# Start of an attention-then-ReGLU kernel: the first k heads in fp32 from the sync engine, w_phi's second copy and batch 0's q by matmul, and a new written order

## The chip, the cores and the metric

The kernel runs on one core of a Trainium2 chip. The metric is device time in microseconds (us). The engines are TensorE (PE, with its weight loads shown as PEld), VectorE (DVE), ScalarE (ACT), GpSimd (POOL) and SyncE (SP). SP, ACT and POOL issue DMA transfers; POOL's can change the type on the way. "The clock" is TensorE's granted clock, 1.00 being full.

## The reference

```python
def phi(x):
    proj = np.einsum('bhsd,df->bhsf', x, w_phi)
    proj = proj - np.max(np.abs(proj), axis=-1, keepdims=True)
    return np.concatenate([np.exp(proj), np.exp(-proj)], axis=-1)
q_p, k_p = (phi(q), phi(k))
kv = np.einsum('bhsf,bhsd->bhfd', k_p, v)
z = np.sum(k_p, axis=2)
num = np.einsum('bhsf,bhfd->bhsd', q_p, kv)
den = np.einsum('bhsf,bhf->bhs', q_p, z)[..., None] + 1e-06
attn = num / den
# x = attn, heads side by side: 4608 tokens x 512
out = (np.maximum(x @ w_gate, 0.0) * (x @ w_val)) @ w_out
```

There are 8 batches, 8 heads, 576 tokens, head size 64 and 128 features in w_phi; the gate and value weights are 512 x 1536, w_out is 1536 x 512. All inputs and the output are fp32 in memory.

## The kernel before, in words

**Tiling.** The 576 tokens of a batch are 512 "full" tokens (four tiles of 128) and 64 "rest" tokens. Heads go in three groups j = 0, 1, 2 of 2, 3 and 3 heads. The rest tokens of k ride along with group 0; the rest tokens of q of two batches together form "mixed" tiles, which make up a ninth block of 512 tokens. Each of the nine blocks (g = 0 to 8) then goes through the FFN: 12 column blocks of value (fv) and gate (fg) with four matmuls of 512 columns each, the product (ga), and four output tiles (fo, three parts each).

**Attention of one batch.** k is turned so that the head size lies on partitions (kt on DVE; in batch 0 k0 on PE, a transpose by matmul, and k1 on DVE, which copies it out). It is projected by w_phi (kr, from the 32-row copy w32; in batch 0 k2, from the 64-row copy w64). From the projection in a bank ACT makes both exponentials (ke, two for each of four token tiles and each group: 24 a batch), DVE the largest absolute value (kx), ACT the factors from it (kk, kp), and POOL, in batch 0 also DVE, scales v by them (vs, vd; vr for the rest tokens, vo and vp for the column of ones). kv sums over tokens on PE (80 matmuls of 65 columns), kc or kd copies it out. q goes the same way (qt on DVE, qc or qs on PE with w32, qe on ACT, qx on DVE); qy, qz, qu and qw make a factor per token. nu is q's product with kv, and nt, nv, nr (DVE) and nx (POOL) scale and normalize it. x is turned by xp and xa in batch 0, by a DMA (xt) elsewhere. In block 0 the FFN's first eight column blocks go tile by tile (pv, pg, pa, pb: 16 matmuls of 128 columns), so that they can begin with the first tile.

**Order.** The order of all work is written out in the string ORDER, some 2,000 words such as `ke.0.1.2.0:2@kp0`: step ke with arguments (batch 0, group 1, tile 2, sign 0), in bank 2, in slot 0 of the buffers kp. Each word calls the function `do_<step>`, and an engine runs its own instructions in the order of the words. There are eight banks of 128 x 512 fp32. Nothing reorders at run time: an instruction that waits holds up what its engine has behind it, and a DMA that waits holds up its issuer.

**The start.** POOL loads k, q and batch 0's v (lk L417, lq L424, lm, lv), bf16 for k and q, then the FFN weights (wl L477: value and gate in thirds; wo L483). SP loads w_phi twice: wp (L373) as 32 rows of pairs for w32, wq (L379) as 64 rows for w64, each in fp32, which wc (L382) and wd (L385) cast on DVE. `zz` are matmuls of zeros (L408, 256 columns) with no use for the result; there are 62. `gt` is a tiny SP load that waits for k of batch 0's first heads. After gt, SP loads v of batch 1 (L459).

The first words of the order before:

```python
ms.0 ms.2 ms.3@vr0 lk.0.1 ms.6 wp wq ms.4@vr1 wd ms.5 lq.0.1 wc id if zz.37:0 k0.1:0 k1.1:0@kT0
zz.5:1 k2.1:0123 lk.0.2 ke.0.1.1.0:1@kp0 ke.0.1.2.0:2 ke.0.1.3.0:3 ke.0.1.0.0:0 qt.0.1@qT0
...
lm.1.0 lv.0.0 ke.0.0.3.1:3 ke.0.0.1.0:0 ke.0.2.0.0:4 lv.0.2 ke.0.0.0.1:2 kk.0.1.0 lm.1.1 wl.1.0
...
nx.0.0@xu0 ke.1.1.3.1:0@kp2 wl.1.1 ke.1.1.0.0:7 nu.0.1.0:2 nt.0.1.0:2@t2 nu.0.2.0:4 xp.0.0:1
```

Of the kernel before, what the change touches and what calls it, by code (L numbers as in the profile page):

```python
# [8 lines left out]
FP32 = mybir.dt.float32  # L9
BF16 = mybir.dt.bfloat16  # L10
AF = mybir.ActivationFunctionType
ALU = mybir.AluOpType
# [4 lines left out]
ms.0 ms.2 ms.3@vr0 lk.0.1 ms.6 wp wq ms.4@vr1 wd ms.5 lq.0.1 wc id if zz.37:0 k0.1:0 k1.1:0@kT0  # L17
zz.5:1 k2.1:0123 lk.0.2 ke.0.1.1.0:1@kp0 ke.0.1.2.0:2 ke.0.1.3.0:3 ke.0.1.0.0:0 qt.0.1@qT0
ke.0.1.3.1:3 kx.0.1.1:1@mk0 lk.0.0 kx.0.1.2:2 ke.0.1.2.1:2 ke.0.1.1.1:1 lm.0.1 zz.6:4 k0.2:4
k1.2:4@kT0 zz.7:5 k2.2:4567 ke.0.2.2.0:6@kp1 kx.0.1.3:3 ke.0.2.3.1:7 lm.0.0 lq.0.0 kx.0.1.0:0  # L20
kx.0.2.0:4@mk1 ke.0.1.0.1:0 lw.0.0 k0.0:2 k1.0:2@kT0 zz.7:1 k2.0:2013 kk.0.1.1@ek0 ke.0.2.1.1:5
qt.0.0@qT1 kx.0.2.3:7 ke.0.2.2.1:6 kx.0.2.2:6 kx.0.0.0:2@mk2 lv.0.1 ke.0.0.2.1:1@kp2 ke.0.2.1.0:5
lm.1.0 lv.0.0 ke.0.0.3.1:3 ke.0.0.1.0:0 ke.0.2.0.0:4 lv.0.2 ke.0.0.0.1:2 kk.0.1.0 lm.1.1 wl.1.0
kx.0.2.1:5 kp.0.2.1:7 ke.0.0.0.0:2 ke.0.2.0.1:4 lw.0.1 qs.0.1.0:6 kx.0.0.1:0 kx.0.0.3:3 qx.0.1.0:6
vs.0.1.1@vs0 kp.0.2.0:7 qs.0.0.1:5 qe.0.0.1.0:5@qp0 gt.0 lk.1.3 qs.0.0.2:2 lv.1.2 kx.0.0.2:1
ke.0.2.3.0:7 vp.2:7@vs1 kk.0.0.1@ek1 vs.0.1.0 ke.0.0.2.0:1 qs.0.0.0:4 wl.0.1 kk.0.0.0 ke.0.0.3.0:3
qx.0.0.0:4 qx.0.0.2:2 vo.0@vs2 vd.0.2.0:7 ke.0.0.1.1:0 qs.0.1.1:1 qe.0.0.1.1:5 qe.0.0.0.1:4@qp1
qx.0.1.1:1 qs.0.1.2:3 qe.0.1.2.0:3@qp2 qe.0.0.0.0:4 qs.0.0.3:0 qe.0.0.3.0:0@qp3 wl.0.0 qe.0.1.0.0:6
qs.0.1.3:4 qx.0.0.1:5 qe.0.0.3.1:0 vd.0.2.1:7 qe.0.1.0.1:6 qe.0.1.1.0:1 vr.0.0.0 vr.0.0.1 qy.0.0:5
qx.0.1.2:3 vr.0.1.0 qx.0.1.3:4 vr.0.1.1 kv.0.2:7 kc.0.2:7@kv0 vo.1 kv.0.1:6 qz.0.0:5@my0 qu.0.0@mz0  # L30
qw.0.0@cq0 qx.0.0.3:0 kt.1.1@kT0 nu.0.0.2:7 nt.0.0.2:7@t0 qe.0.1.3.1:4 qy.0.1:0 qz.0.1:0@my0
vs.0.0.1 kc.0.1:6 ku.1@kT1 vs.0.0.0 kv.0.0:5 qe.0.1.3.0:4 nu.0.0.1:6 nt.0.0.1:6@t1 kc.0.0:5
qe.0.0.2.0:2 qu.0.1@mz0 qw.0.1 qy.0.2:0 qe.0.1.1.1:1 nv.0.0.1:6@u0 qe.0.1.2.1:3 qy.0.3:4 nu.0.0.0:5
nt.0.0.0:5@t2 qe.0.0.2.1:2 nv.0.0.2:7 nv.0.0.0:5 nr.0.0@r0 nu.0.1.1:1 qz.0.2:0@my0 qu.0.2@mz0 lv.1.0
nt.0.1.1:1@t2 qz.0.3:4@my0 nu.0.1.2:5 qw.0.2 nv.0.1.1:1@u1 lq.1.2 nt.0.1.2:5@t0 kr.1.1:7630
nx.0.0@xu0 ke.1.1.3.1:0@kp2 wl.1.1 ke.1.1.0.0:7 nu.0.1.0:2 nt.0.1.0:2@t2 nu.0.2.0:4 xp.0.0:1
xa.0.0:1 nv.0.1.2:5 nv.0.1.0:2 wo.0 nu.0.2.1:5 nr.0.1@r0 nx.0.1@xu0 kx.1.1.3:0@mk2 wl.0.2 nu.0.2.2:2
lm.2.0 nt.0.2.1:5@t2 ke.1.1.3.0:0 nt.0.2.2:2@t0 nt.0.2.0:4@t1 ke.1.1.1.1:6 lm.2.1 qu.0.3@mz0
kx.1.1.2:3 pv.1.0:1 pa.1.0:1@val0 ke.1.1.1.0:6 nv.0.2.0:4@u1 nv.0.2.1:5 nv.0.2.2:2 nr.0.2@r0
pg.0.0:0 nx.0.2@xu1 kx.1.1.0:7 kx.1.1.1:6 qw.0.3 xp.0.1:1 nu.0.3.1:4 xa.0.1:1 ke.1.1.0.1:7  # L40
# [12 lines left out]
fv.0.10:0 va.0.10:0@val3 fv.0.11:2 lk.2.3 qe.1.0.0.1:5 va.0.11:2@val0 qx.1.0.1:3 kr.1.2:0476
kx.1.2.0:0@mk2 ke.1.2.3.0:6@kp1 pg.1.3:5 fg.0.11:2 kx.1.2.2:7 kx.1.2.3:6 qe.1.0.1.0:3 ke.1.2.1.1:4
kx.1.2.1:4 ke.1.2.2.0:7 qe.1.0.3.1:1 ku.2@kT1 ke.1.2.0.1:0 pb.1.3:5 kk.1.2.0@ek2 ke.1.2.2.1:7
fv.0.9:3 va.0.9:3@val1 fg.0.8:1 ke.1.2.1.0:4 wo.1 lv.2.3 ga.0.11:2 vr.1.0.0 qy.1.0:7 qz.1.0:7@my0
mt.0 fg.0.10:5 ga.0.8:1 kk.1.2.1 ke.1.2.0.0:0 vs.1.0.1 mc.0:4732 me.0.2.0:3 mx.0.3:2 me.0.0.0:4
qu.1.0@mz0 mx.0.2:3 me.0.0.1:4 vr.1.1.1 vo.1.0 kv.1.0:0 kc.1.0:0@kv1 ga.0.10:5 mx.0.0:4 qw.1.0@cq0
mx.0.1:7 vs.1.1.1 kv.1.1:1 me.0.2.1:3 kc.1.1:1 nu.1.1.0:0 nt.1.1.0:0@t2 fg.0.9:5 vo.1.2@vs1 lv.2.0
kt.2.1@kT0 vs.1.2.1 nu.1.0.0:1 me.0.3.1:2 ga.0.9:5 ke.1.2.3.1:6 nu.1.0.1:4 nu.1.1.1:3 nt.1.1.1:3@t0  # L60
nt.1.0.0:1@t1 vs.1.2.0 kv.1.2:6 nv.1.1.0:0@u0 nv.1.1.1:3 me.0.1.0:7 kt.2.0 lw.2.1 fo.0.1.0:5
kc.1.2:6 nu.1.0.2:6 nt.1.0.2:6@t0 nu.1.1.2:3 nt.1.0.1:4@t2 me.0.3.0:2 nu.1.2.0:2 nt.1.2.0:2@t3
nv.1.0.0:1@u1 me.0.1.1:7 lq.2.2 nv.1.0.2:6 nv.1.0.1:4 nr.1.0@r0 nv.1.2.0:2@u2 fo.0.1.1:5 fo.0.1.2:5
oc.0.1:5@ob0 nt.1.1.2:3@t2 nu.1.2.2:4 nt.1.2.2:4@t3 lw.2.0 nv.1.1.2:3 nr.1.1@r1 kr.2.0:2617
# [196 lines left out]
def kernel(  # L261
# [805 lines left out]
```

## Time and profile before

| | |
|---|---|
| three runs | 379.4, 379.1, 378.24 us; median 379.1 |
| the profiled execution: its time | 378.79 us |
| its span (first to last instruction) | 376.8 us |
| mean granted clock | 0.986 |
| busy: PE, DVE, ACT, POOL | 367.3, 296.3, 222.6, 161.4 us |
| DMA | 38.04 MB, mean 101 GB/s |
| FFN matmuls of 512 columns (L916, L977) | 1,220 recorded, 379 ns each from start to modelled end |
| ke (L563), 192 | 513 ns each |
| qe (L709), 128 | 632 ns each |

Matmuls are pipelined: a matmul of 512 columns is recorded with 379 ns, but the next one starts 216 ns later, so four of them take 0.86 us in the chain of waits. On ACT and DVE too, instructions in a row overlap a little; ten ke take 3.95 us together. The page's slices divide the span in 40 parts, each digit being the busy share in tenths. Windows give busy times of each engine in a stretch that one names. The chain of waits goes back from the last instruction, at each step to what released it. The time of an execution is a little more than its span; the 2.0 us around it are not part of the program's instructions.

### The profile page before, as it was taken

To read this page: it belongs to the slowest core of one execution; us is meant where nothing else is said; L and a number is where in the kernel's file an instruction comes from. 1 tells how busy PE (TensorE), PEld (TensorE's weight loads), DVE (VectorE), ACT (ScalarE), POOL (GpSimd) and SP (SyncE) were. 2 spreads that over 40 slices of the span, in tenths; PEclk is the share of its full clock that TensorE was granted. 3 is DMA by queue.
4 is the path that set the end of the run, shared out by engine and by line. 5 is a ranking of instruction groups with operands and counts; after the bars stand their busy time and mean duration, and the time that the engine had idled before them with its cause. 6 is when DMAs were issued, how large, how long until landed. Compare 5 with 4: busy or idle time off the path is not lost.

```text
span 376.8 us, 9181 instructions
## 1 busy us (share of the span) xinstructions
PE 367.3 (97%) x3591; PEld 197.2 (52%) x3591; DVE 296.3 (79%) x680; ACT 222.6 (59%) x539; POOL 161.4 (43%) x180
## 2 busy tenths in 40 slices
PE   8788999999999999999999999999999999999996
PEld 6457857546544645455435554464444644444443
DVE  3989999989996899989989898888876657642351
ACT  1988996998578544776586547755774400302111
POOL 7777595595477042581475233812341212200000
PEclk9859999999999999999999999999999999999999
DMA  9999999699954664289713944193400021301122
GB/s 126 235 200 220 148 176 152 112 129 143 122 118 58 147 72 113 57 138 91 103 64 37 189 120 99 35 155 92 86 28 3 2 70 57 91 22 29 28 57 111
DMA packets 90513, 38.04 MB, mean 101 GB/s; under 512 B 64230, under 2 KB 85734, under 8 KB 90470
## 3 DMA queue, kind: packets, MB, share of 16 engines
q0 software_dynamic: 33904, 15.23, 31.2%
q1 hardware_dynamic: 56422, 22.10, 27.7%
q8 instruction: 28, 0.46, 0.6%
q10 hardware_dynamic: 144, 0.13, 0.1%
q14 instruction: 15, 0.12, 0.1%
HBM read 37.95 MB, written 9.44 MB: 126 GB/s over the span
## 4 chain that ended last, share of the span: by engine, by line
PE 89%; DVE 5%; ACT 4%; DMA 2%; issue 0%; SPq 0%; DVEq 0%; ACTq 0%
PE bank L916 46%; PE bank L977 22%; PE bank L658 6%; PE bank L757 4%; PE bank L945 4%; PE bank L694 3%; ACT kp L563 2%; PE bank L511 2%; DMA w64f<-in_w_phi_dram 2%; DVE mk L571 1%; ACT qp L709 1%; PE bank L1006 1%; PE bank L898 1%; DVE u L788 1%; DVE maxq L717 1%; DVE t L778 1%
## 5 line engine op out<-in xcount | busy, mean ns | idle before, releaser
L563 ACT ACTIVATE kp<-bank 128x384 bf16<-128x384 f32 x192 | 83.2, 513 | 26.2 <-PE bank L511 15.0
L977 PE MATMUL bank<-wo,h 128*128 128x512 bf16 x420 | 98.3, 379 | 0.0
L937 DVE SCALAR_TENSOR_TENSOR h<-bank,val 128x512 bf16<-128x512 f32 x100 | 66.3, 681 | 29.8 <-PE bank L916 25.5
L916 PE MATMUL bank<-xTs,wg 128*128 128x512 bf16 x352 | 86.7, 379 | 0.0
L916 PE MATMUL bank<-xTs,wv 128*128 128x512 bf16 x352 | 86.2, 379 | 0.0
L800 POOL TENSOR_TENSOR xu<-u,r 128x512 bf16<-128x512 f32 x36 | 37.5, 1044 | 97.3 <-DVE r L796 92.4
L931 ACT CAST val<-bank 128x512 bf16<-128x512 f32 x70 | 41.6, 606 | 62.2 <-PE bank L916 50.8
L709 ACT ACTIVATE qp<-bank 128x512 bf16<-128x512 f32 x128 | 70.9, 632 | 10.1 <-DVE maxq L717 5.1
L618 POOL TENSOR_TENSOR vs<-vn,ek 128x780 bf16<-128x780 f32 (+3 forms) x40 | 53.0, 1338 | 37.8 <-ACT ek L580 35.1
L977 PEld LDWEIGHTS <-h 128*128 128x128 bf16 x420 | 39.1, 98 | 44.0 <-issue 0.9
L916 PEld LDWEIGHTS <-wv 128*128 128x128 bf16 x400 | 37.0, 98 | 43.2 <-issue 3.5
L916 PEld LDWEIGHTS <-wg 128*128 128x128 bf16 x400 | 37.4, 98 | 42.0 <-issue 1.8
L571 DVE TENSOR_REDUCE mk<-bank 128x3 f32<-128x384 f32 x96 | 49.0, 539 | 4.3 <-ACT kp L563 2.2
L717 DVE TRANSPOSE_TENSOR_REDUCE maxq<-bank 128x16 f32<-128x512 f32 x64 | 42.3, 692 | 3.5 <-PE bank L694 2.3
L986 ACT COPY ob<-bank 128x512 f32<-128x512 f32 x23 | 13.6, 593 | 37.5 <-PE bank L977 37.2
L788 DVE TENSOR_TENSOR u<-bank,t 128x195 f32<-128x195 f32 (+1 forms) x108 | 33.4, 330 | 1.9
L778 DVE TENSOR_TENSOR t<-bank,cq 128x195 f32<-128x195 f32 (+1 forms) x96 | 29.8, 327 | 5.0 <-PE bank L757 4.1
L757 PEld LDWEIGHTS <-qp 128*128 128x128 bf16 x512 | 24.1, 98 | 13.6 <-issue 2.0
L757 PE MATMUL bank<-kv,qp 128*128 128x65 bf16 x512 | 27.2, 194 | 1.2 <-ACT qp L709 0.8
L934 DVE CAST val<-bank 128x512 bf16<-128x512 f32 x30 | 20.2, 678 | 8.4 <-PE bank L916 8.3
L658 PEld LDWEIGHTS <-kp 128*128 128x128 bf16 x640 | 24.0, 101 | 3.7 <-DVE h L937 0.3
L658 PE MATMUL bank<-vs,kp 128*128 128x65 bf16 x512 | 24.2, 199 | 0.0
(88 smaller groups left out, 357.0 us busy)
## 6 DMA issues: line engine op xcount, KB each, us to landing
out_dram<-ob SPq DMA_DIRECT2D x31, 256.0 KB, 2.2
vn<-in_v_dram SPq DMA_DIRECT2D x24, 256.0 KB, 5.4
kn<-in_k_dram POOLq DMA_DIRECT2D x7, 512.0 KB, 6.4
qn<-in_q_dram POOLq DMA_DIRECT2D x7, 512.0 KB, 7.6
wg<-in_moe_w_gate_dram POOLq DMA_DIRECT2D x3, 512.0 KB, 8.5
wv<-in_moe_w_val_dram POOLq DMA_DIRECT2D x3, 512.0 KB, 10.0
wo<-in_moe_w_out_dram POOLq DMA_DIRECT2D x3, 512.0 KB, 8.7
out_dram<-ob SPq DMA_DIRECT2D x9, 128.0 KB, 2.4
```

Source lines behind the costliest of these rows:

```text
L563: nc.scalar.activation(kp_of(3 * b + j)[:, i, s].rearrange("p n f -> p (n f)"), bank[bk[0]][:, 0 : 3 * F], AF.Exp, scale=(1.0, -1.0)[s],)
L571: nc.vector.tensor_reduce(mk_of(3 * b + j)[:, :, i], bank[bk[0]][:, 0 : 3 * F].rearrange("p (n f) -> p n f", f=F), axis=AX.X, op=ALU.max, ...
L618: nc.gpsimd.tensor_tensor(vs_of(3 * b + j)[:, s, 0:n].rearrange("p n i e -> p (n i) e")[:, :, 0:e], src[:, lo:hi].rearrange("p h i e -> p ...
L658: nc.tensor.matmul(out_ps[:, h - lo, s, :], lhsT=lhsT, rhs=rhs, start=(at == 0), stop=(at == 2 * n * (C + 1) - 1),)
L709: nc.scalar.activation(qp_of(4 * b + i)[:, s, 4 * hq : 4 * hq + 4].rearrange("p h m -> p (h m)"), bank[bk[0]], AF.Exp, scale=(1.0, -1.0)[s],)
L717: nc.vector.tensor_reduce(maxq[:, :, i, 4 * hq : 4 * hq + 4].rearrange("p t h -> p h t"), bank[bk[0]].rearrange("p (h t u) -> p h t u", h= ...
L757: nc.tensor.matmul(bank[bk[0]][:, E * n : E * (n + 1)], lhsT=qp_of(4 * b + i)[:, s, h, :], rhs=kv_of(b)[:, h, s, :],)
L800: eng.tensor_tensor(xu_of(n).rearrange("p (h d) -> p h d", d=D), u_of(n)[:, :, 0:D], r_of(n).to_broadcast([P, H, D]), op=ALU.mult,)
L916: nc.tensor.matmul(bank[bk[0]], lhsT=w[:, dc, P * f : P * f + P], rhs=xT(g)[:, dc, :], start=(dc == 0), stop=(dc == NDC - 1),)
L931: nc.scalar.copy(val_of(NFC * g + f), bank[bk[0]])
L937: nc.vector.scalar_tensor_tensor(h2_of(g, f), bank[bk[0]], 0.0, val_of(NFC * g + f), op0=ALU.max, op1=ALU.mult)
L977: nc.tensor.matmul(bank[bk[0]], lhsT=h2_of(g, f)[:, P * t : P * t + P], rhs=wo_sb[:, f, :], start=(f == 0), stop=(f == NFC - 1),)
```

## The change

- **lf, cf, cg**: k of batch 0's heads 2 to 4 comes in fp32 by one SP DMA, the first on that queue, into the memory of the mixed block's x (not yet in use); DVE casts two heads to bf16 and ACT one. The POOL load lk.0.1 goes.
- **wr**: the 64-row copy of w_phi is loaded from ACT's queue and no longer from SP's.
- **sl, w1, wa**: the 32-row copy is no longer loaded. sl (DVE) writes a selection matrix from the identity; w1 (PE, two matmuls) picks the rows from w64 into a bank; ACT copies them to w32. This stands ahead of batch 1's first projection.
- **q0, q1, qb**: batch 0's q is turned by PE (8 transposes of 128 columns for four heads, copied out by DVE) and projected from w64 by one matmul of 512 columns per tile and half, where two matmuls with w32 did it. Its four token tiles now hold every fourth token, so the output rows of block 0 are written with a stride of four.
- **vq**: the scaling of v for the rest tokens, both signs in one POOL instruction (16 for 32).
- **zz**: 17, 3, 5 and 4 in place of 37, 5, 6, 7 and 7.
- **Order**: all words are in a new order, and some evictions change engine (va 69 for 70, vb 31 for 30, oc 26 for 23, oe 9 for 12, kc 17 for 19, kd 7 for 5). do_lu, do_qv, and do_wc's new form are defined and not called.

```diff
-    w32f = sb.tile([P, 2, F], FP32, name="w32f", tag="w32f")
+    sel = sb.tile([D, 2, P], BF16, name="sel", tag="sel")
...
-    def do_wp(bk):
-        nc.sync.dma_start(
-            out=w32f.rearrange("p a f -> p (a f)"),
-            in_=w_phi.rearrange("(r a) f -> r (a f)", a=2)[None].to_broadcast([4, R, 2 * F]),
-        )
+    def do_sl(bk):
+        nc.vector.tensor_copy(
+            sel.rearrange("d a (i r) -> d a i r", r=R),
+            ident[0:D, 0:D].rearrange("d (r a) -> d a r", a=2)[:, :, None, :].to_broadcast([D, 2, 4, R]),
+        )
+
+    def do_w1(bk):
+        for a in range(2):
+            nc.tensor.matmul(
+                bank[bk[0]][:, F * a : F * (a + 1)],
+                lhsT=sel[:, a, :],
+                rhs=w64[0:D, :],
+                start=(a == 0),
+                stop=(a == 1),
+            )
...
+    def do_wr(bk):
+        nc.scalar.dma_start(out=w64f, in_=w_phi[None].to_broadcast([2, D, F]))
...
+    def do_wa(bk):
+        nc.scalar.copy(w32.rearrange("p a f -> p (a f)"), bank[bk[0]][:, 0 : 2 * F])
...
+    def k_first():
+        flat = xT_mix.rearrange("p a b -> p (a b)").bitcast(FP32)[:, 0 : 3 * C * D]
+        return flat.rearrange("p (h x) -> p h x", h=3)
+
+    def do_lf(bk):
+        lo, hi = HEADS[1]
+        nc.sync.dma_start(
+            out=k_first().rearrange("p h (c d) -> p h c d", d=D),
+            in_=k[0, lo:hi, 0:SF, :].rearrange("h (p c) d -> p h c d", c=C),
+        )
+
+    def cast_first(copy, half):
+        lo, hi = ((0, 2), (2, 3))[half]
+        at = HEADS[1][0]
+        copy(
+            kn_of(0)[:, at + lo : at + hi].rearrange("p h c d -> p h (c d)"),
+            k_first()[:, lo:hi],
+        )
+
+    def do_cf(bk, half):
+        cast_first(nc.vector.tensor_copy, half)
+
+    def do_cg(bk, half):
+        cast_first(nc.scalar.copy, half)
...
+    def do_vq(bk, b, hh):
+        r = slice(SM * hh, SM * (hh + 1))
+        nc.gpsimd.tensor_tensor(
+            vr_of(b)[r, :, :, hh, :],
+            vm_of(b)[r][:, None, :, :].to_broadcast([SM, 2, 4, E]),
+            ek_of(3 * b)[r, :, 0, :][:, :, :, None].to_broadcast([SM, 2, 4, E]),
+            op=ALU.mult,
+        )
...
+    def do_q0(bk, hq):
+        pt = bank[bk[0]].bitcast(BF16)
+        for n in range(8):
+            h, cp = 4 * hq + n // 2, n % 2
+            nc.tensor.matmul(
+                pt[:, P * n : P * n + P],
+                lhsT=qn_of(0)[:, h, 2 * cp : 2 * cp + 2, :].rearrange("p c d -> p (c d)"),
+                rhs=ident,
+                is_transpose=True,
+            )
+
+    def do_q1(bk, hq):
+        nc.vector.tensor_copy(
+            qT_of(hq).rearrange("p h m a -> p (h m a)"), bank[bk[0]].bitcast(BF16)
+        )
...
+    def do_qb(bk, hq, i):
+        T = qT_of(hq).rearrange("p h m a -> p (h m a)").rearrange("p (h k m) -> p h k m", k=2, m=P)
+        r = slice(D * (i % 2), D * (i % 2 + 1))
+        nc.tensor.matmul(bank[bk[0]], lhsT=w64[r, :], rhs=T[r, :, i // 2, :], start=True, stop=True)
...
             dst = out[S * g + P * t : S * g + P * (t + 1), :]
+            if g == 0:
+                dst = out[0:SF, :].rearrange("(p c) n -> p c n", c=C)[:, t]
```

The start of the new order, up to the first gate matmuls (lines in between left out):

```python
ms.0 id if ms.3@vr0 lf ms.4@vr1 ms.5 wr ms.2 cf.0 wd sl cg.1 lk.0.2 zz.17:0 k0.1:0 k1.1:0@kT0 zz.3:1
k2.1:0123 ke.0.1.0.1:0@kp0 ke.0.1.3.1:3 ke.0.1.0.0:0 ms.6 k0.2:4 kx.0.1.1:1@mk0 k1.2:4@kT0
ke.0.1.2.1:2 kx.0.1.3:3 kx.0.1.0:0 lq.0.0 ke.0.1.1.0:1 lm.0.0 ke.0.1.3.0:3 zz.5:5 k2.2:4567
...
qe.0.0.1.0:6 qz.0.0:3@my0 qu.0.0@mz0 kv.0.2:7 kt.1.1@kT0 qy.0.3:6 kc.0.1:1@kv0 lq.1.2 vo.0 vs.0.0.0
qe.0.0.3.0:5@qp3 kv.0.0:2 qz.0.3:6@my0 qw.0.0@cq0 qu.0.3@mz0 nu.0.0.1:1 kc.0.2:7 nt.0.0.1:1@t0
kc.0.0:2 qy.0.1:3 qz.0.1:3@my0 qe.0.1.2.1:0 qu.0.1@mz1 qe.0.1.3.0:4 qe.0.1.2.0:0 nv.0.0.1:1@u0
wl.1.0 nu.0.0.2:7 nu.0.0.0:2 nt.0.0.0:2@t1 nu.0.1.1:6 qw.0.1 w1:3 wa:3 nt.0.0.2:7@t0 nv.0.0.0:2
...
qe.0.0.3.1:5 nu.0.1.2:0 nt.0.1.2:0@t2 nv.0.1.0:2@u1 qe.0.1.3.1:4 zz.4:7 kr.1.1:1375 nv.0.1.2:0
...
xp.0.1:1 qw.0.3 ke.1.1.2.0:7 qt.1.1@qT1 xa.0.1:1 lv.1.1 pv.0.0:0 lv.1.3 pa.1.0:4@val0 lm.1.0
kx.1.1.2:7 pv.0.1:1 ke.1.1.1.0:3 nx.0.2@xu0 pa.0.0:0@val1 pa.0.1:1@val2 kt.1.0@kT0 nu.0.3.1:4
nt.0.3.1:4@t0 ke.1.1.3.0:5 pg.0.1:2 pb.0.1:2 qc.1.1:1065 wl.0.2 ke.1.1.1.1:3 ke.1.1.2.1:7 ln.0.1
```

More of the change, by code (lines that the diff above doesn't have):

```diff
@@ L462, in do_lv, with do_lu @@
             )
+    def do_lu(bk, i):
+        lo, hi = HEADS[i]
+        nc.sync.dma_start(
+            out=v_flat()[:, lo:hi],
+            in_=v[0, lo:hi, 0:SF, :].rearrange("h (p c) d -> p h c d", c=C),
+        )
     def do_gt(bk, j):
```

472 lines of the change are left out of this document (231 added, 241 removed).

## The prediction

> **What bounds the kernel now.** I read the 40 slices of the page first, then the windows, then the chain of waits, then the timeline of the first 10 us.
>
> ```profile
> PE   8788999999999999999999999999999999999996
> ...
> PEclk9859999999999999999999999999999999999999
> DMA  9999999699954664289713944193400021301122
> ```
>
> One slice is 9.4 us. TensorE (PE) is full from the fifth slice on; before it PE is not full and its clock drops to half in the third. The windows put numbers on that:
>
> ```profile
> 29.90:89.10 59.20, 58.71 (x839) 38.52 (x841) 57.05 (x144) 52.97 (x132) 44.43 (x50) 1.00 1.02 149
> 89.10:373.65 284.55, 284.50 (x2516) 142.95 (x2514) 216.87 (x488) 149.10 (x355) 95.49 (x97) 1.00 0.46 81
> ```
>
> The columns are length, then busy time of PE, PE's loads, VectorE (DVE), ScalarE (ACT) and GpSimd (POOL), clock, DMA. From 29.90 (the first batch-1 projection, step kr.1.1) to 373.65 (the last matmul) PE is busy 343.21 of 343.75 us. DVE, 57.05 of 59.20, is the second limit up to 89.10. So the end is the moment when this run begins, plus 343.75, plus 3.15 (to the end of the span at 376.8). Only the 29.9 us ahead can shrink; the rest can only grow. The chain of waits says what orders the start:
>
> ```profile
> 1.56 6.35 DMA w64f<-in_w_phi_dram
> 9.72 3.95 ACT kp L563 x10
> 13.77 3.06 ACT kp L563 x8
> ```
>
> First w_phi's 64-row copy is awaited till 7.91; then the exponentials of k go back to back on ACT, which is full (10.00 of 10 us between 10 and 20) and 8.69 of the next 10. The first exponential, 9.72, is therefore the handle. What lies between 7.9 and it:
>
> ```profile
> 7.65 0.50 PE L533 MATMUL bank<-ident,kn 128*128 128x128 bf16 x6
> ...
> 7.94 0.23 DVE L385 CAST w<-w64f 128x128 bf16<-128x128 f32 x1 [4.60 <-DMA w64f<-in_w_phi_dram]
> ...
> 8.22 0.35 DVE L382 CAST w<-w32f 128x256 bf16<-128x256 f32 x1
> 8.49 0.21 DVE L391 CAST identf<-ident 128x128 f32<-128x128 bf16 x1
> 8.62 0.54 DVE L536 COPY kT<-bank 128x768 bf16<-128x768 bf16 x1
> ...
> 9.23 0.51 PE L554 MATMUL bank<-w,kT 64*128 64x128 bf16 x12 [0.53 <-DVE kT L536]
> ```
>
> The first k was there in time (its transposes at 7.65 show no DMA wait), but DVE stands at w64f and has three more steps (a memset and two casts) ahead of the copy of kT.
>
> **Start of k (lf, cf, cg, wr, sl).** Removed: the w32f DMA of 128 KB and the first k DMA on POOL, two steps of DVE (0.35, and identf's 0.21 moved into idle time). Added: lf, 3 heads x 512 x 64 x 4 B = 384 KB, first on SP (0.74). Its landing was never seen in this form. Lower end: output stores of 256 KB take 2.2 us to land, x1.5 = 3.3, so 4.0. Upper end: v by SP into xTs takes 7.6 us for 256 KB under full load, x1.5 = 11.4, so 12.1. Nearest row: the same 384 KB of k, by POOL, issued at 1.25, beside w_phi and q; the kn row gives 4.7 us as the shortest of four (the next, 7.0, would end at 8.25, after the transposes began), so 5.95. I take 5.0 for lf, landing at 5.8 (estimate): q's 512 KB no longer run beside it, but the k of heads 5 to 7 soon does. wr, 64 KB on the empty ACT queue, lands before that; d1's ACT store of 128 KB takes 1.7.
>
> The Trainium skill, "Trainium Kernel Development and Optimization", Key Constraints, holds that DMAs from SP, ACT and POOL run on the same 16 engines and that several issuers save issue time only. The DMA row above (nine tenths from the first slice) agrees; by it the landing would be POOL's 5.95 less half a microsecond of earlier issue, 5.4 (an estimate), and the sum below -1.8 instead of -1.4.
>
> Then cf.0 on DVE: 128 columns take 0.23 and 256 take 0.35, so 512 take 0.60: 6.4; cg.1 (256 columns, ACT's 0.37) lies beside it. wd and sl (0.23 and about 0.3) lie beside the six transposes. These take 0.50 and the projection 0.51 at full clock; at half clock I add 0.25 to each. Which clock? The next windows are 3.41 us each:
>
> ```profile
> 2.90:6.31 3.41, 3.41 (x18) 2.35 (x16) 0.43 (x1) 0.00 (x0) 3.33 (x8) 1.00 1.12 170
> ...
> 13.14:16.55 3.41, 1.59 (x20) 0.70 (x19) 3.41 (x8) 3.41 (x11) 1.53 (x2) 1.00 1.04 228
> 16.55:19.96 3.41, 2.97 (x9) 0.59 (x10) 3.10 (x7) 3.41 (x14) 3.37 (x5) 0.50 1.20 195
> ...
> 23.38:26.79 3.41, 3.41 (x65) 3.41 (x64) 3.05 (x6) 2.17 (x6) 2.92 (x4) 0.50 1.23 203
> ```
>
> The clock fell to 0.50 after a window busy for 1.59, stayed there through one of 2.97, and came back after a full one (3.41), at 26.79. The opening zero matmuls go from 37 to 17; 16 loads fall into the first of these windows, 0.21 us each, so 17 end at 1.06 + 3.6 = 4.7, and the PE idles for lf until 6.4. I expect half clock there. So: 6.4 + 0.75 + 0.54 (copy of kT) + 0.76 = 8.45 for the first exponential, 1.27 earlier (1.77 at full clock).
>
> **Batch 0 after that.** The number of exponentials is unchanged (24 of k, 16 of q), so ACT keeps the gain if it is fed. K of heads 5 to 7 was issued at 3.51 behind q; now it is POOL's first DMA, behind the identity. On DVE the two transposes of q (1.10 and 1.09) become two copies of 1024 columns (0.54 x 4/3 = 0.73 each): 0.7 saved. On PE 16 matmuls of 512 columns become 8 and 16 transposes of 128: 3.5 to 2.6 us at 0.216 and 0.056 each, which lies beside full ACT, worth 0; uncovered it would be 0.9. Of DVE's 0.7 I count 0.3, since DVE and ACT both were nearly full up to 28. Added at the edge of the full run: two matmuls of w1 (0.11), 4 zero matmuls (0.44), and wa on ACT (0.37); kr.1.1 waits for wa, and ACT's queue and the exponentials of batch 1 stand behind it. I count 0.2 of them. Sum at the start: -1.27 - 0.3 + 0.2 = -1.4 us.
>
> **Elsewhere, 0.** vq: 16 POOL products of twice the width for 32 of 0.62 us; the 128x520 product takes 1.06, so 17 for 19.6 us, on an engine that waits 92 us for DVE's r alone. Evictions change engine: DVE gets one val and two kv more, three ob and two others fewer, about -1.6 us; ACT gets about 1.5 more, which its 149 of 284 busy us hide; in the stretch to 89.10 they would show. Batch 0's output rows are strided by 4 but are still 2 KB each. No instruction is dropped by "no bank kept". From kr.1.1 on the steps are the same, apart from those named; their order is new throughout.
>
> **DMA and queues.** SP: lf, then gt.0 and vm and four loads of v behind it, as before. POOL issues the first gate weights (wl.1.0) only after the last product of v, about 23.9 (25.42 less 1.5), instead of at 12.41; with 8.5 us to landing that is 32.4. Their first user, pg.0.1, follows pv.1.0 (about 32.2 - 1.4 = 30.8) after some 3 us of PE work, 33.8. 1.4 us of cover; beyond that PE stands, in order, microsecond for microsecond.
>
> **Sum.** The profiled execution has a span of 376.8 and a time of 378.79 (2.0 around it); -1.4 gives 377.4. The median of the three runs, 379.1, lies 0.3 higher and gives 377.7. I say **377.5**. About 0.3% (1.14 us) is what a measurement can tell from no change.
>
> **Rivals.**
> - *k lands early*: lf at 4.0, by the store row. First exponential at 6.65, 3.1 earlier: 375.7. Against it: DMA is full from the first slice. Chance 0.10.
> - *Gain eaten on the way*: wl.1.0 lands like wv's 10.0 instead of 8.5, at 33.9, and DVE (96% busy up to 89) holds the new order up for the rest; or lf, sharing its engines with wr and the k of heads 5 to 7, lands at 7.0 and the first exponential stays at 9.7. About 378.9. For it: 1.4 us of cover is thin. 0.27.
> - *Half clock in the full run* (slower): the 80 matmuls of kv take 4.4 us at half clock (55 ns each, from the timeline), so they fill a whole counting window only if they begin less than 1.0 us ahead of its edge. In the trace they began at 23.3, 0.1 before one. If they miss it, and PE between is under the 2.97 that did not restore it, half clock lasts up to two windows of full work, 6.8 us, and costs half, 3.4: net +2.0, 381.1. It decides at a loss of over 2.5 us. 0.15. The Trainium skill, "TensorE: Matmul & The Clock Gate", Part 1, says that the window is 3.4 us and free-running, not tied to the kernel's start; the spacing of the windows above agrees, and the phase cannot be predicted.
> - *lf late*: as v into xTs; landing at 10, first exponential 12.65, 2.9 later: 382. Slower by 0.3% from a landing at 9.7. 0.08.
>
> **Chances.** Forecast 0.40, early 0.10, eaten 0.27, half clock 0.15, late 0.08. Faster 0.50, same 0.27, slower 0.23. The range leaves out half of the early case and most of the late one: 375.6 to 381.2; the forecast's own is 376.6 to 378.0.
>
> **What would show it.** lf's landing (DVE's wait ahead of cf) at 5.8; first exponential at 8.45; half clock from the start till after kv; PE full from about 30.5 with no wait for wg; PE busy over 99.5% from there to the end; the same 3.15 us of tail. It is wrong if PE has idle time over 1.5 us after 31, or if the first exponential is not ahead of 9.

## The result, and the profile after

The kernel after takes 381.7 us (median of 19 runs, 379.95 to 383.78), the kernel before 378.95 (19 runs beside them, 378.16 to 380.0): 1.0065 times as long, 95% interval 1.005 to 1.0081. It is slower by some 2.5 us, where 377.5 and faster was forecast. The profiled execution has a time of 381.75 and a span of 379.9 us. One execution of a run below (e1), at 423.8 us with a mean clock of 0.84, was slow throughout and is left out of its median.

The slices of the page of the kernel after, one 9.5 us:

```profile
PE   7598998969999999999999999999999999999996
...
PEclk9689999999999999999999999999999999999999
DMA  9999899690966946596075295014442002200132
```

The half clock has moved from the third slice to the second. But the seventh and ninth slices of PE, nines before, are 8 and 6. Windows from the first batch-1 projection (kr.1.1, now at 26.92) to the last matmul, cut at the same distance as before (columns as in the prediction's: length, busy PE, PE's loads, DVE, ACT, POOL, clock, DMA share and rate):

```profile
26.92:86.12 59.20, 52.90 (x777) 35.01 (x777) 51.99 (x131) 47.84 (x120) 32.91 (x38) 1.00 0.98 147
86.12:376.88 290.76, 290.22 (x2568) 145.85 (x2566) 220.98 (x496) 154.88 (x370) 104.04 (x96) 1.00 0.44 81
```

So the sum of the prediction can be filled in: 26.92 + 349.96 + 3.07 = 379.95, where it was 29.88 + 343.77 + 3.13. The start gained 2.96 us, the dense stretch (from the first batch-1 projection to the last matmul) lost 6.19, the tail is as it was. The gain at the start is that of one execution: in the traces of five runs below whose words are the same up to there (e2, e3, e5, e7, e10), this projection came at 27.11 to 28.02, and with the start of before (e4, e14) at 29.84, so the gain is 1.8 to 3.0 us. PE is busy 343.1 us in the dense stretch now and was 343.2 before; what was added is waiting, with 52.90 of 59.20 us busy in the first window. PE's four longest waits behind 28.5 us (total, times, longest):

```profile
PE bank L996 <- issue: 3.2, 1, 3.2
PE bank L1025 <- DVE t L858: 1.4, 1, 1.4
PE bank L558 <- DVE kT L547: 1.3, 1, 1.3
PE bank L996 <- ACT ob L1066: 0.5, 1, 0.5
```

Together they are 6.36 us, where the trace of before had one of 0.35 in this stretch. The names to the right of the arrow are only the last to be seen; behind each stands a DMA. The profile gives the times from the issue of these DMAs to their landing:

```profile
wg<-in_moe_w_gate_dram POOLq DMA_DIRECT2D x1, 512.0 KB, 11.2
km<-in_k_dram POOLq DMA_DIRECT2D x1, 32.0 KB, 6.3
kn<-in_k_dram POOLq DMA_DIRECT2D x1, 512.0 KB, 7.4
xTs<-xu SPq DMA_TRANSPOSE x1, 5.9
```

- **wg**, the first third of the gate weights, sent at 22.55, landed at 33.72; PE stood from 32.36 to 33.77.
- **km**, batch 2's key tails (lm.2.1 at 54.95, lm.2.0 at 57.46), landed at 63.75; the turn ku.2 began at 63.84, and PE stood from 62.95 to 64.21 for kr.2.0. Before, these two loads had gone out at 34.19 and 34.91, thirty us ahead of their use at 64.4.
- **xTs**, the last transposed tile of batch 1 (xt.1.3), sent at 73.04, landed at 78.89; PE stood from 75.77 to 78.98 for the first products of FFN group 1. Beside it **kn**, batch 3's keys, had gone out on POOL at 72.87. Before, the same transpose took 2.44 us (71.08 to 73.52), with the keys sent two us behind it.
- The fourth: a store of an output tile (od.0.2) behind two transposes on SP, sent 115.70, landed 119.50; ScalarE waited for its buffer and PE 0.48 us for ScalarE.

The chain of waits of the kernel after passes through three of them (start, length):

```profile
54.95 8.80 DMA km<-in_k_dram x2
...
64.21 0.57 PE bank L558 x24
...
77.51 1.47 issue
78.98 3.18 PE bank L996 x14
...
115.70 3.79 DMA out_dram<-ob
```

At 77.51 it says "issue", where the times above show the landing at 78.89 behind the wait.

The start, VectorE's and ScalarE's timeline of the kernel after:

```profile
4.06 0.66 DVE L451 CAST kn<-xTm 128x512 bf16<-128x512 f32 x1 [0.16 <-DMA xTm<-in_k_dram]
5.52 0.40 DVE L400 CAST w<-w64f 128x128 bf16<-128x128 f32 x1 [0.80 <-DMA w64f<-in_w_phi_dram]
...
5.97 0.53 DVE L583 COPY kT<-bank 128x768 bf16<-128x768 bf16 x1
```
```profile
7.05 3.17 ACT L610 ACTIVATE kp<-bank 128x384 bf16<-128x384 f32 x8 [2.58 <-PE bank L601]
```

The fp32 keys were there at 4.04, w_phi's copy was what DVE awaited, until 5.52, and the first exponential came at 7.05, 2.67 us ahead of before.

### The profile page after: what moved, and what is told of

It reads as the page before. It is cut to its first block, busy times and chain, and to the rows that moved or that the text cites. A ratio compares the mean times of both kernels' runs of the same rounds, so it can differ in the third digit from the quotient of the medians.

```text
span 379.9 us, 9112 instructions
## 1 busy us (share of the span) xinstructions
PE 362.8 (95%) x3568; PEld 193.6 (51%) x3568; DVE 295.9 (78%) x679; ACT 224.2 (59%) x543; POOL 157.7 (41%) x163
## 3 DMA queue, kind: packets, MB, share of 16 engines
HBM read 37.81 MB, written 9.44 MB: 124 GB/s over the span
## 4 chain that ended last, share of the span: by engine, by line
PE 82%; DMA 5%; DVE 5%; ACT 4%; POOL 2%; issue 2%; SPq 0%; POOLq 0%; DVEq 0%; ACTq 0%
PE bank L996 45%; PE bank L1057 19%; PE bank L714 5%; PE bank L837 3%; PE bank L1025 3%; ACT kp L610 3%; DMA km<-in_k_dram 2%; PE bank L558 2%; PE bank L774 2%; DMA qn<-in_q_dram 2%; DVE u L868 1%; DVE t L858 1%; DMA out_dram<-ob 1%; DVE mk L618 1%; DVE qT L765 1%
## 5 line engine op out<-in xcount | busy, mean ns | idle before, releaser
L1011 ACT CAST val<-bank 128x512 bf16<-128x512 f32 x69 | 40.6, 597 | 65.1 <-PE bank L996 46.1
L789 ACT ACTIVATE qp<-bank 128x512 bf16<-128x512 f32 x128 | 69.9, 626 | 11.8 <-PE bank L774 7.6
L1066 ACT COPY ob<-bank 128x512 f32<-128x512 f32 x26 | 15.3, 594 | 38.9 <-PE bank L1057 29.7
L1014 DVE CAST val<-bank 128x512 bf16<-128x512 f32 x31 | 21.2, 682 | 7.1 <-PE bank L996 6.0
## 6 DMA issues: line engine op xcount, KB each, us to landing
wg<-in_moe_w_gate_dram POOLq DMA_DIRECT2D x3, 512.0 KB, 11.2
```

The lines of the kernel that those rows point to most:

```text
L789: nc.scalar.activation(qp_of(4 * b + i)[:, s, 4 * hq : 4 * hq + 4].rearrange("p h m -> p (h m)"), bank[bk[0]], AF.Exp, scale=(1.0, -1.0)[s],)
L1011: nc.scalar.copy(val_of(NFC * g + f), bank[bk[0]])
```

## Experiments

All are timed against the kernel before, in the same job.

| run | what | median us | ratio to before, 95% |
|---|---|---|---|
| e1, e7 | after, km early | 381.7, 381.9 | 1.0067 (1.0051 to 1.0083), 1.0080 (1.0063 to 1.0097) |
| e5 | after, keys of batch 3 early | 378.70 | 0.9992 (0.998 to 1.0004) |
| e2 | after, both | 377.74 | 0.9960 (0.9948 to 0.9972) |
| e3 | e2, store early, gate product later | 377.54 | 0.9962 (0.9947 to 0.9977) |
| e4 | before, km late | 383.22 | 1.0120 (1.010 to 1.014) |
| e14 | before, keys beside the transpose | 379.53 | 1.0004 (0.9988 to 1.0021) |
| e10 | after, wait filled | 382.82 | 1.0094 (1.0075 to 1.0112) |
| e6 | e2, first keys by POOL | 378.67 | 0.9993 (0.9985 to 1.0002) |
| e12 | e6, table loaded early | 378.74 | 0.9981 (0.9968 to 0.9995) |
| e11 | before, w_phi early, fewer fillers | 378.59 | 0.9981 (0.997 to 0.9993) |
| e8, e9, e13 | new start, old dense order | 388.9, 382.4, 382.0 | 1.0263 (1.0241 to 1.0286), 1.0081 (1.0059 to 1.0103), 1.0069 (1.0041 to 1.0096) |

### The waits of the new order, undone one by one

e1 moves two words of the order, e2 a third as well, e3 a pair and one store besides:

```diff
 e1   ... wl.1.2 ku.1 ...
+lm.2.1 lm.2.0
 lk.2.3 ...                          (both taken from behind wo.2)
 e2   ... lq.2.2 ... ku.2
+lk.3.3
 lm.3.1 ...                          (taken from behind nx.1.3, xt.1.3)
 e3   ... xp.0.2:3
+pg.0.1:2 pb.0.1:2                   (taken from ahead of qc.1.1)
 ...
+od.0.2
 xt.2.3 ...                          (taken from behind xt.2.2)
```

> The kernel after, with one thing moved: the two loads of batch 2's key tails (km) go out on POOL ahead of the load of batch 2's keys at about 40 us, instead of at 54.95 and 57.46. Theory A (single late landings): in the kernel after, TensorE waited 1.26 us at 62.95 for the first scores of batch 2, because km landed at 63.75; that wait goes, the scores start near 63, and the last normalised tile of batch 1, which ScalarE and VectorE reach sooner too, shortens the next wait (3.21 us at 75.77) by one to two more. Median 379.4, between 378.6 and 380.5. Theory B (the engines behind TensorE are the bound from 64 to 77): the idle time only moves to 75.8, and the median stays at 381.3 to 381.9.

> As the run before, and the load of batch 3's keys (1 MB read, 512 KB written) moved on POOL from 72.87, where it ran beside the last transposed tile of batch 1 on the way to TensorE (issued 73.04, landed 78.89, 5.85 us where others took 2.4 to 4.4), to about 60.6, right behind the load of batch 2's queries. Theory A: that tile lands some 3 us after its issue, and the wait of 3.21 us at 75.77 goes whole: median 377.2, between 376.5 and 378.5. Theory B: the tile is late because its normalisation (POOL, 71.88) is late, and at most 1 us more than in the run before comes off: 379 or over.

> As the run before, with two more: the store of an output tile that stood on SP behind two transposes (issued 115.70, landed 119.50, TensorE waiting 0.48 us at 119.73) goes ahead of them at about 110; and the first gate product of the first FFN part (which waited 1.41 us at 32.36 for its weights, landed 33.72) goes on TensorE behind a query product and a transpose that have their inputs by then (0.57 + 0.22 us). Theory A: 0.48 and up to 0.8 come off: median 376.0, between 375.3 and 377.5, faster than the kernel before. Theory B: no more than 0.3 comes off.

e1 gained nothing, as theory B had it. e2 gave 4.0 us (1.05% between the two ratios), nearly all that theory A wanted, and beats both kernels. e3 added nothing that can be told from e2, as its theory B had it, though the wait for the store is gone from its trace. In e2 the transpose, sent at 72.76, landed at 75.20:

```profile
xTs<-xu SPq DMA_TRANSPOSE x1, 2.4
```

and PE's longest waits behind 28.5 us, 6.36 in the kernel after, came down to 2.1 (three):

```profile
PE bank L1025 <- DMA wg<-in_moe_w_gate_dram: 0.8, 1, 0.8
PE bank L996 <- DVE mk L618: 0.7, 1, 0.7
PE bank L996 <- ACT ob L1066: 0.6, 1, 0.6
```

Two more runs tell why e1 gained nothing: e5 has the second move alone, and e7 is e1's kernel again.

> The kernel after with only the second move of the run e2: the load of batch 3's keys goes out on POOL at about 60.6 instead of at 72.87; the two loads of key tails stay where the kernel after has them. Theory A (the waits add up): the wait of 1.26 us for the key tails stays, the 3.21 us at 75.77 goes: 378.9, between 378.2 and 379.6. Theory C (the last transposed tile alone sets that stretch, the wait for the tails lies in its shadow): as e2, 377.7, between 377.0 and 378.4.

> The kernel of e1 once more, for its trace. It had the median of the kernel after, so Theory B's number held there. Theory C: no wait at 62.95 is left, the last transposed tile of batch 1 is again issued beside the load of batch 3's keys and lands some 5.8 us later at about 78.5 to 79, and TensorE waits about 4 us for it in place of 1.26 and 3.21. Theory B proper (ScalarE and VectorE bind that stretch): the idle time is spread over several waits for these engines.

e5 came out where A had it, 378.7: the keys' load is 2.8 of the 4.0 us. But its trace has no wait for km at all. There km landed 4.5 us after its issue, at 62.10, in e10 below 4.4 us after, in the kernel after 6.3, though the three orders are the same up to there; so the wait of 1.26 us belongs to some executions only, which alone could make e1 worth little. That e5 met A's number is therefore luck: the wait that A let stay is not there, and of the one that was to go, half is.

e2 is still 1.2 us (0.32%) faster than e5, with the scores of batch 2 at the same time (62.99, 63.06). The two traces show 0.8 us of it, which is also the difference of their spans (376.3, 377.1): for the same last transposed tile PE waited 0.74 us in e2, and in e5

```profile
PE bank L996 <- DVE mk L618: 1.5, 1, 1.5
```

In e5 the transpose took its 2.4 us but went out 0.87 later (73.63 for 72.76). The order puts the last normalisation of batch 1 (nx.1.3) into the buffer of the first (xu0), so POOL can begin it only when the first transposed tile has landed: 71.53 in e2, 72.40 in e5, the normalisation 0.16 us behind in both, and in the kernel after and e7 too (71.72 and 71.88, 69.91 and 70.07). With the key tails sent early, POOL sends the queries of batch 2 and the keys of batch 3 0.8 us sooner, and these keys landed at 67.59 in e2, at 69.82 in e5, where that first transpose, beside them, took 6.35 us for 5.57. So e1's move pays once the keys are out of the way of the last transpose. Neither the buffer nor this order of loads was changed alone.

e7 shows where the rest of e1's gain went. There is no wait at 62.95; the transpose goes out at 71.14, 1.9 us sooner than in the kernel after, beside the keys at 71.06; it takes 6.0 us, and PE stands from 74.07 to 77.21. Then the windows of the clock:

```profile
74.34:77.75 3.41, 0.54 (x3) 0.32 (x4) 2.77 (x5) 2.22 (x5) 1.63 (x2) 1.00 1.34 202
77.75:81.16 3.41, 3.41 (x10) 1.22 (x8) 0.21 (x1) 0.82 (x2) 0.12 (x1) 0.50 0.99 186
```

A window with 0.54 us of work, and the next at half clock: 3.41 us that do 1.7 us of work. In the kernel after, the wait from 75.77 to 78.98 lay across the edge at 77.11, and neither part brought the clock down. So in this execution the 1.8 us that PE resumed sooner were paid back at half clock; 299.8 us from there to the last matmul against 297.9 in the kernel after. Theory C was right in that the wait stayed one wait for the transpose (3.1, not 4 us); the clock was in nobody's expectation. Theory B's number was right; its reason, ScalarE and VectorE, is not seen: nearly all of the idle time is one wait, ended by the landing.

### The same two things done to the kernel before

```diff
 e4   ... lq.2.2
+lm.2.1 lm.2.0                       (taken from behind wl.0.2)
 ...
+ku.2                                (taken from some 85 words ahead)
 kr.2.0:2617 ...
 e14  ... nx.1.3@xu1
+lk.3.3                              (taken from behind xt.1.3)
```

> The kernel before with the late order of the kernel after put into it at one place: the two loads of batch 2's key tails go out on POOL at about 60.5, behind the load of batch 2's queries, instead of at 34.19, and the turn of the tails on VectorE just ahead of the first scores of batch 2 (64.4 us). Theory A: the tails land at about 66.5, TensorE waits some 2.4 us for them, and the end moves by that or more: median 381.3, between 380.5 and 383. Theory B (such a wait is made good behind it, since the engines behind TensorE bound that stretch): within 0.7 of before, 379.0 to 379.7.

> The kernel before with the collision of the kernel after put into it: the load of batch 3's keys goes out on POOL directly behind the last normalisation of batch 1 (at about 71.05, instead of 73.13), so beside the transpose that carries this tile (issued 71.08, landed 73.52, 2.44 us). Theory K (a load of 1 MB on POOL's queue beside a transpose on SP's holds the transpose up: 5.85, 5.98 and 5.94 us in after, e7 and e10, 2.42 to 2.44 in e2, e3 and e5, where the load was away): the tile lands at about 77.0, the first product of the next FFN group, at 75.36 before, waits 1.6 us, and the median rises by that, to 380.8 (380.2 to 381.8). Rival (the transpose was slow for its place behind other work on SP): lands by 74.5, within 0.4 of before.

e4 lost 4.1 us in the median and 4.4 in the span, more than A's 2.4. The wait is there, near the 2.4 us expected:

```profile
PE bank L511 <- DVE kT L500: 2.9, 1, 2.9
```

The rest is again the clock: the window from 63.77 to 67.18 held 0.69 us of matmuls, and the next ran at half clock, 1.7 us. 2.87 + 1.7 is 4.6; the spans differ by 4.4 (381.2 for 376.8).

e14 lost nothing. The transpose was held up, but by half of what K said, 4.24 us for 2.44:

```profile
xTs<-xu SPq DMA_TRANSPOSE x1, 4.2
```

It landed at 75.46, and PE came to it at 75.59: the old order had two us of other work there. So the load of keys beside the transpose costs what lies beyond this cover. In the kernel after, e7 and e10 the transpose took 5.85, 5.98 and 5.94 us, there with the keys sent 0.1 to 0.2 us ahead of it, in e14 0.08 behind. There is a second difference: in the kernel after, e7 and e10 two loads of v (256 KB each) go out on SP itself 1.2 to 1.3 us behind the transpose, in e14 none goes out before it lands. In e2 these loads go out as far behind it, without the keys, and the transpose took 2.4; so they don't hold it up by themselves. Which of the two makes the difference between 4.2 and 5.9 was not tried.

e10 fills the wait of the kernel after with work that changes nothing, to test the clock's part in its spread of times:

```diff
+zz.26:0
 fg.1.3:0 fv.1.3:1
```

> The kernel after with 26 products of the zero tile on TensorE (about 2.9 us at full clock; they add nothing to the output) ahead of the gate product that waits 3.21 us for the last transposed tile of batch 1. No wait is taken away; TensorE is only busy while it lasts. Theory G (a wait of 2 us and more in one 3.41 us window of the clock makes the next window run at half clock, as behind the waits of e4, e7 and e8; so half of the runs of the kernel after lose up to 1.7 us more than its profiled run): the runs above 381 go, median 380.3, between 379.8 and 380.8. Rival (the spread of the kernel after comes from elsewhere): unchanged at 381.4 to 382.0, or later by what of the fillers runs past the landing.

Theory G fell: all five runs are at 382.4 to 383.3, none below the median of the kernel after. The trace has no half clock behind the fill, PE goes on at 77.6 when the tile has landed, and then meets two more late stores (waits of 0.99 at 118.36 and 1.13 at 153.34). What spreads the runs of the kernel after from 380 to 383.8 was not found.

### What the start is worth, and to what

e6 is e2 with `lf cf.0 cg.1` taken out and `lk.0.1` as POOL's first load; e12 adds to it

```diff
+    def do_ta(bk):
+        nc.scalar.copy(mark[:, 0:8], zero[:, 0:8])
...
-ms.5 wr ms.2 wd
+ms.5 wr ta ms.2 wd
```

and e11 is the kernel before with `wp wq` and `zz.37` made `wq wp` and `zz.24`, and `wc` behind the first exponentials.

> The run e2 with the first part of the change undone: heads 2 to 4 of batch 0's keys come through POOL's queue (cast on the way, first of its loads) instead of in fp32 through SP with two casts on the chip. By the traces of before and after the first keys land at about 6.4 instead of 4.04 and POOL's other loads go out 0.9 us later; theory A: the first exponential goes from 7.05 to about 8.9, all of the start with it, and the median rises by 1.7 against e2, to 379.4 (378.8 to 380.2). Rival: ScalarE, full from 10 to 20 us, has other work to put first and the tails of the start hide it: under 0.6 us, 378.3 or less.

> The run e6 (keys of heads 2 to 4 through POOL again) with a copy of 128x8 zeros on ScalarE at the very start, which nothing reads. In e6 the scores came only 0.26 us later than in e2, the first exponential 1.09 later, since the load of ScalarE's table (1.28 us) stood ahead of it; in e2 the cast of the keys on ScalarE had drawn it forward to 1.91. Theory T: with the table loaded early the first exponential comes at about 7.3, and the median is within 0.4 of e2: 377.9, between 377.6 and 378.2. Rival (the fp32 way itself is worth it): 378.5 to 378.8 as e6.

> The kernel before with w_phi alone made early: of its two copies of w_phi on SP the 64-row one, which VectorE awaited until 7.94 us, goes first, the cast of the other moves behind the first turn of keys, and 24 instead of 37 filler products stand ahead of the first keys. Keys still come through POOL (landed 6.35). Theory W (the filler products, which ended at 7.8, and the copy of w_phi held the start, not the keys' way): the first exponential goes from 9.72 to about 8.2, the start with it by 1.0 to 1.5, median 377.7, between 377.3 and 378.1. Rival (the keys' landing held it): under 0.3, 378.6 to 379.2.

e6 lost 1.25 us (0.33%) against e2: between its two numbers. Its scores came at 6.83, only 0.26 behind e2's 6.57, but ScalarE had its table still to load:

```profile
6.86 1.28 ACT L610 ACT_TABLE_LOAD   x1 [6.86 <-DVE kT L583]
8.15 1.25 ACT L610 ACTIVATE kp<-bank 128x384 bf16<-128x384 f32 x3
```

In the kernel after and e2 the cast cg.1 draws this load to 1.91. e12 draws it to 1.90 too, and the first exponential to 7.51. Yet the first batch-1 projection came at 28.62, for 28.75 in e6 and 27.61 in e2, and the time did not fall below e6's range: theory T is not borne out. Of the fp32 way's 0.8 to 1.2 us, at least a part comes later than the first exponential. The trace of e12 shows where: its chain of waits goes back to the second half of batch 0's queries, which POOL loads.

```profile
6.59 6.87 DMA qn<-in_q_dram
...
13.50 0.63 PE bank L745 x8
...
14.23 0.70 DVE qT L753
...
14.97 0.63 PE bank L763 x2
```

ScalarE, which has no such wait in e2 and e5, waited 0.51 us, from 15.08 to 15.59, for the projections of these queries. They landed at 13.45, for 11.95 in e2: POOL, with the first keys to load too, sent them 0.73 later, and they were 0.78 longer under way. e3 has the same wait (0.46 us at 14.62, queries landed at 12.94) and the latest first batch-1 projection of the five traces named above, 28.02. The chain of the kernel after goes through this load as well, from 5.83 to 12.15.

So ahead of the dense stretch the first exponential is not the only handle; how much of the 0.8 to 1.2 us these queries make was not tried alone. POOL's loads of v are the rival; they landed 1.0 to 1.6 us later in e6 and e12 than in e2 (lv.0.1 at 11.64 and 12.17 for 10.64, lv.0.2 at 18.18 and 18.59 for 16.95). But in e5 they landed at 11.33 and 17.68, near e6's, and its first batch-1 projection still came at 27.46, for 28.75 in e6.

e11 brought the first exponential of the kernel before from 9.72 to 8.48,

```profile
8.48 0.87 ACT L563 ACTIVATE kp<-bank 128x384 bf16<-128x384 f32 x2 [6.47 <-PE bank L554]
```

the first batch-1 projection from 29.88 to 29.31, and 0.19% of the time, 0.7 us: half of theory W's. There the keys, landed at 6.78, were next.

### The new start with the old dense order

> The start of the kernel after, word for word up to the first scores of batch 1, and behind it the order of the kernel before (1869 steps; 34 of them with another bank or buffer number), so the new start without the new order; the gate weights' first third goes out ahead of batch 1's queries, since the old order wants them sooner. Theory A (the new dense order lost the gain): first scores of batch 1 at 27 to 28 us instead of 29.9, behind it 343.8 us as before, under 1.5 us of waits in the dense part: median 376.6, between 376.0 and 377.5. Rival (the gain can't be had, since the loads of weights and queries for the stretch from 30 to 36 us come no sooner): waits of 2 to 3 us there, median 378.5 to 379.5.

> The run e8 with its seam mended. There the old order let VectorE turn the key tails of batch 1 at 28 us, while the new start's POOL sends their load only at 23.35 (landed 33.71): VectorE stood 5.3 us, TensorE 5.48 us, and two windows of half clock followed (32.2 to 39.0). Here that turn stands just ahead of its first use, some 12 us later; nothing else differs. Theory A (the old dense order keeps the gain of the new start): first scores of batch 1 at 27.1 to 28.1, under 2 us of waits behind them: 376.9, between 376.0 and 378.0. Rival (weights and queries for 30 to 36 us can't land in time behind the new start): waits of 2 us and more, 378.5 or over.

> The run e9 with the fault of its seam taken out: there the loads of batch 2's key tails stood ahead of the turn of batch 1's in the one buffer, so that POOL waited 3.6 us to overwrite it (its normalisations behind that wait, and TensorE 1.47 and 1.90 us behind them) and the turn read batch 2's tails for batch 1. Here they go out behind that turn, ahead of the load of batch 2's keys, as in e1. Theory A (the old dense order keeps the gain of the new start): waits behind the first scores under 2 us, median 377.0, between 376.2 and 378.2. Rival (an order laid out for a later start doesn't fit an earlier one, whatever single load is mended): 379.5 or over, as the waits for the first weights (1.1 us at 31 to 34) stay and others come.

In e8 VectorE stood in order at ku.1 until 34.3 for a load that its new start sends late. e9 moves this word behind the next loads of the same buffer, so that the turn works on batch 2's tails in place of batch 1's, and POOL waits 3.6 us before it may overwrite the buffer. e13 has neither:

```diff
 e9   ... 
+ku.1                                (from the place that the old order gives it, some 90 words ahead)
 kr.1.0:2573 ...
 e13  (as e9)
+lm.2.0 lm.2.1                       (from behind wl.0.2)
 lk.2.3 ...
```

All three are slower than the kernel before; theory A is refuted in e13, with its start at 27.01 and still 382.0. Its main waits on PE:

```profile
PE bank L1026 <- ACT val L1041: 2.6, 2, 1.9
PE bank L997 <- DVE h L1047: 1.4, 1, 1.4
```

They lie at 37.92 and 58.06. At the first, four exponentials of q stand ahead of the copy that frees PE's bank; PE starts this stretch 2.9 us sooner than before, batch 1's queries land at 33.28, only 1.4 sooner than before (34.71), and half clock follows from 39.76 to 43.17. So the old order, which ran almost without waits behind its own start, met them behind an earlier one in all three. That the new order as such is bad is not shown: the new order with three loads moved (e2) is the one that keeps most of the gain.

## Why the prediction was wrong

- **"Only the 29.9 can shrink; the rest can only grow"** held: 29.88 went to 26.92, 343.77 grew to 349.96.
- **"Elsewhere, 0 ... their order is new throughout"** is the step that failed. It costed the steps and not their order. The waits at 62.95, 75.77 and 119.73 are 4.95 of the 6.19 us in the profiled execution; moving three loads, which took away the first two waits, gave 4.0 us of the time back (e2). All three can be read from the order itself: lm.2.1 and lm.2.0 stand 46 and 15 words ahead of ku.2, where before it was 140 and 146; lk.3.3 is POOL's next word behind nx.1.3, whose tile xt.1.3 carries; od.0.2 stands behind two transposes. The sign that was named for it, "PE idle over 1.5 us after 31", is what came.
- **wl.1.0, "32.4, with 1.4 us of cover"**: it landed at 33.72, sent 1.35 us sooner than forecast (22.55 for 23.9) but 11.2 us under way for 8.5, and since the start was quicker PE came at 32.36, not 33.8. This part of the rival "gain eaten" (33.9, "microsecond for microsecond") was right, 1.41 us, though its 33.9 was made of a later issue and a shorter way. Its second mechanism, DVE as the holder of the new order, was not: e2 takes the waits away without touching DVE.
- **lf, "5.8"**: 4.04, the lower end, by the row of the stores; 3.3 us for 384 KB. The term was mis-sized by 1.8 us; it took for nearest the keys that POOL loads among others, while this DMA was the first on SP, ahead of POOL's. That row was misread too: its 4.7 us are those of the tiny load gt.0, which it also holds; the keys' own load took 5.10 and landed at 6.35, not 5.95. The Trainium skill, "DMA: Bandwidth & Descriptors", Anatomy of one DMA, fits 2.0 us plus the bytes at 436 GB/s to POOL's DMAs, 2.9 us here (an estimate). For this load, from SP, the run gives 3.3, 0.4 more.
- **"First exponential 8.45"**: 7.05. The clock came up sooner than forecast: the transposes of the first keys still took 0.80 us at 4.78, but from 5.43 it was full, until 12.26, then half until 22.50 (before: full from 6.31 to 16.55, half until 26.79). Of the 2.67 us the first exponential gained (2.4 against e4 and e14, where the old start had it at 9.44), w_phi and the fewer fillers give 1.24 where they are alone (e11; 0.96 against 9.44). The forecast named only lf as the handle, and lf was not the last to be awaited; w64f was, as before.
- **Batch 0, "-0.3"**: from the first exponential to the first kv matmul 13.27 us for 13.57, -0.30. **"+0.2" at the edge**: from there to kr.1.1 6.60 for 6.59, nothing. That the first came out to the hundredth is luck: in e2, e3, e5, e7 and e10 this stretch took 13.00 to 13.67 us, and the landing of batch 0's second queries, which the chain of waits goes through (5.83 to 12.15), has no term in the sum.
- **The tail, 3.15**: 3.07.
- **The rival "k lands early"** had nearly the right start (lf 4.0; 3.1 us gained, 2.96 in the profiled execution) and the wrong end, for the same missing term.
- **The rival "half clock in the full run"** did not come in the kernel after, where kv began; but it came behind waits in e4, e7, e8 and e13, which the prediction did not name.
- **The rival "lf late", "slower by 0.3% from a landing at 9.7"**: by the sum's own steps, 2.65 us from lf's landing to the first exponential, this loss begins at a landing of some 8.4. Nothing turned on it.
- **e2's 377.7 beside the forecast's 377.5** is no confirmation of the sum. In its trace the start gained 2.27 us, not 1.4, and the dense stretch lost 1.88, not 0. The spans differ by 0.45 us (376.32 for 376.77); that the medians lie 1.4 apart is not that sum.

## What to carry to other kernels

Where an order is new throughout, work out the lead of each load from its issue to its first user in the new order, against the slowest landing of that row and not the median, and do it again for the start that the change is to make earlier. A transfer that PE needs next should have no large load sent beside it. Time won ahead of a full engine counts only as far as every landing behind it moves too; and a wait that one profile shows may be absent from the next execution (km's was, in e5 and e10), so weigh a mend by timed runs and not by that wait.

## What the runs showed of the hardware

- A transpose of 128x512 bf16 by DMA from SP landed in 2.4 us where no load of keys (1 MB read, 512 KB written) was sent within 2 us of it (before, e2, e3, e5), in 4.24 with that load sent on POOL 0.08 us behind it (e14), and in 5.85 to 5.98 with it sent 0.1 to 0.2 us ahead and two loads of v behind on SP (after, e7, e10). The Trainium skill, "DMA: Bandwidth & Descriptors", Queues, rings and completion order, says that each DMA engine goes round its queues packet by packet. If each of two busy queues got half by that, the transpose would take up to 4.9 us (an estimate, twice the 2.44): the 4.24 fits, the 5.9 is longer.
- Half clock followed 3.41 us windows in which PE's matmuls were busy for 0.46 (e8), 0.54 (e7), 0.69 (e4), 1.57 (e13), 1.59 (before) and 2.09 us (8.84 to 12.26 in the kernel after); it did not follow 1.55 and 2.07 (the two windows of the wait in the kernel after). A wait of 1.9 us was enough in e13 and not in e9, and one of 3.2 across an edge was not in the kernel after. The two sets overlap, so no bound on the busy time can be read from them.
- The first use of ScalarE for arithmetic cost 1.28 us of table loading, and it came at 6.86, behind the wait, in e6, where ScalarE's first instruction was a DMA issue, but at 0.73, ahead of the wait, in the kernel before.
- The same load of 32 KB (lm.2.0) landed 6.3, 4.5 and 4.4 us after its issue in three orders that differ only behind it (after, e5, e10).
